# First unit's products ahead of the second unit's scans, counts behind the last unit's products, and fewer dummy matmuls

## The chip, the cores and the metric

The kernel runs on one core of one Trainium2 chip. The metric is the device time of one execution in microseconds; the time of a kernel is the median over its runs. TensorE (PE), VectorE (DVE), ScalarE (ACT), GpSimd (POOL) and SyncE (SP, which here only issues loads) each work through a queue of their own in order, and wait for each other through semaphores.

## The reference

A linear attention with decay over 4 sequences of 768 tokens and 8 heads of 48, then a routed mixture of 8 experts of equal capacity, then a gated second layer:

```python
for t in range(S):
    cur = np.einsum('bhd,bhe->bhde', u[None] * kt, vt)
    y[:, :, t] = np.einsum('bhd,bhde->bhe', rt, state + cur)
    state = wt[:, :, :, None] * state + np.einsum('bhd,bhe->bhde', kt, vt)
...
logits = x @ w_gate                  # the highest scores first, each expert takes at most N/E tokens
h = np.maximum(x[mask] @ w1[e], 0.0)
out[mask] = h @ w2[e]
...
h = x @ w_in
g = h * np.clip(h + 3.0, 0.0, 6.0) / 6.0
return g @ w_out
```

## The kernel before

The attention is cut into 24 units (6 chunks of 128 tokens by 4 sequences; unit n is chunk n // 4 of sequence n % 4). A loop over n writes out one stage per unit by hand, and the order in which a stage calls its helpers is the order of each engine's queue. A unit goes through these helpers:

- `scans(n)` on DVE: a reversed running product `Q` of the decays, the chunk's whole decay `G`, a reciprocal, and the forward scan `Ap`. It is called two stages ahead.
- `khrh(n)`: `kh` = keys times `Q`, `rh` = queries times `Ap`, each on POOL or DVE. `bonus(n)`: `rk` = keys times queries.
- `cc(n)` on PE: the bonus term from `rk`, into the PSUM tile `pu`, of which there is one; `cc_ev(n)` on ACT copies it out.
- `tr(n)` (transposes of `kh`) and `vp(n)` (values times gate weights) on PE, into the PSUM tile `pk`, of which there is one; `vp_ev(n)` and `tr_ev(n)` on ACT copy it out.
- `scores(n)` on PE: products of `kh` and `rh` into two PSUM tiles `sc`; `scores_ev(n)` on DVE masks them into `P`.
- `seed(n)` on ACT starts the output tile `py` (two of them) with the bonus; `ymm(n)` on PE adds the state's part and `P` times the values; `umm(n)` on PE makes the state's update, `sadd(n)` on DVE adds it, `decay(n)` on POOL scales the state.
- `logits(n)` on DVE sums the gate's part of `py`; `xev(n)` on ACT copies the output, `xst(n)` stores it. `check(n)` on ACT looks at the range of the decays (two passes, line 226 and 227).

Stage n calls, on PE: dummy matmuls, `tr(n)`, `vp(n)`, `scores(n)`, then `ymm(n-1)`, `umm(n-1)` and `cc(n+1)`. The dummies multiply a tile of ones (`wz`) into `pk`, where the next products overwrite them; their number per stage stands in `WARMS` (line 65), the last entry for all later stages, and with three more from unit 20 on (line 408). Ahead of the loop, 13 dummies run while the first loads come in, and units 0 and 1 are prepared.

The routing needs counts of tokens by score and expert. `compare8(u)` on DVE writes a comparison `cm` for 128 tokens, `top` on DVE the best expert `oh`, and `sum8(u)` on PE adds their product into `cnt` (two small matmuls each, line 629). The list `counted` holds those that wait for their `sum8`; it is emptied at the end of the stages 22 and 23 and behind the loop's two extra stages 24 and 25.

Behind the loop every engine branches around `stepwise` (line 518), a path for decays out of range. Then the experts' part begins: the search for the thresholds of the first expert on DVE and PE (its first step is `sat`, line 688), the gather of its tokens, and a long stretch of matmuls for 8 experts in which PE is busy nearly all the time. Second-layer weights are decoded on the side: ACT takes an absolute value (line 862), POOL clamps it (line 865).

Of the kernel before, what the change touches and what calls it, by code (L numbers as in the profile page):

```python
# [9 lines left out]
F32 = mybir.dt.float32  # L10
# [5 lines left out]
ALU = mybir.AluOpType  # L16
# [3 lines left out]
B, H, S, D = 4, 8, 768, 48  # L20
CH = 128
NCH = S // CH
NU = B * NCH
# [7 lines left out]
R = 112  # L31
CW = NP * (CH + 1) + 1
# [29 lines left out]
LASTWAIT = 24  # L62
KEPT = 16
COUNT8 = {22: (16, 17), 23: (18, 19), 24: (), 25: ()}
WARMS = 0, 6, 3, 6, 5, 5, 5, 5, 4
F64LO = 2.0 ** -15
F64HI = float(np.uint32(0x47EFFFFF).view(np.float32))

# [1 line left out]
class Kernel:  # L70
# [77 lines left out]
    def attention(self):  # L148
        tc, nc, t = self.tc, self.nc, self.t
        with ExitStack() as ctx:  # L150
# [6 lines left out]
            ps_k = ctx.enter_context(tc.tile_pool(name="ps_k", bufs=1, space=PSUM))  # L157
# [9 lines left out]
            KH = [A.tile([128, NP, CH], F32, name=f"KH{i}") for i in range(3)]  # L167
            RH = [A.tile([128, NP, CH], F32, name=f"RH{i}") for i in range(3)]
# [3 lines left out]
            T = {}  # L172

            def ok(q):
                return 0 <= q < NU
# [24 lines left out]
            def scans(n):  # L200
                d = T[n]
                w = d["w"]
                Q = d["Q"] = wk.tile([R, CW], F32, tag="Q", name=f"Q{n}", bufs=2)
                Ap = d["Ap"] = wk.tile([R, CW], F32, tag="Ap", name=f"Ap{n}", bufs=2)

                nc.vector.tensor_tensor_scan(Q[:, ::-1], w[:, ::-1], top[:R, 0:1].to_broadcast([R, CW]), 1.0, op0=ALU.mult, op1=ALU.min)
                d["G"] = io.tile([R, NP], F32, tag="G", name=f"G{n}", bufs=8)
                nc.vector.scalar_tensor_tensor(d["G"], Q[:, 1:CW - 1:CH + 1], 1.0e-30, top[:R, 0:1].to_broadcast([R, NP]), op0=ALU.max, op1=ALU.mult)
                yield

                nc.vector.reciprocal(w[:, 0:CW - 1:CH + 1], d["G"])
                yield
                nc.vector.tensor_tensor_scan(Ap[:, 0:CW - 1], w[:, 0:CW - 1], top[:R, 1:2].to_broadcast([R, CW - 1]), 1.0, op0=ALU.mult, op1=ALU.add)

            def khrh(n, eng, eng2=None):
                d = T[n]
                d["kh"], d["rh"] = KH[n % 3], RH[n % 3]
                q = d["Q"][:, 1:CW].rearrange("p (a b) -> p a b", b=CH + 1)[:, :, 1:]
                a = d["Ap"][:, 0:CW - 1].rearrange("p (a b) -> p a b", b=CH + 1)[:, :, :CH]
                eng.tensor_tensor(d["kh"][:R], d["kr"][:, 0], q, op=ALU.mult)  # L220
                (eng2 or eng).tensor_tensor(d["rh"][:R], d["kr"][:, 1], a, op=ALU.mult)

            def check(n):
                jk = wk.tile([R, NP, CH], BF16, tag="jk", name=f"jk{n}", bufs=2)
                wv = T[n]["w"][:, 0:CW - 1].rearrange("p (a b) -> p a b", b=CH + 1)[:, :, 1:]
                nc.scalar.activation(jk, wv, AF.Relu, bias=cb[:, 0:1], scale=-1.0, accum_out=acc[:, 2 * n:2 * n + 1])
                nc.scalar.activation(jk, wv, AF.Relu, bias=cb[:, 1:2], scale=1.0, accum_out=acc[:, 2 * n + 1:2 * n + 2])

            def bonus(n):

                d = T[n]
                d["rk"] = wk.tile([R, NP, CH], F32, tag="rk", name=f"rk{n}")
                (nc.vector if n < 2 else nc.gpsimd).tensor_tensor(d["rk"], d["kr"][:, 0], d["kr"][:, 1], op=ALU.mult)

            def cc(n, pu):
                d = T[n]
                d["pc"] = pu[:, 448:448 + H]
                for p in range(NP):
                    nc.tensor.matmul(pu[:, 448 + 2 * p:450 + 2 * p], d["rk"][:, p], UB[:, 2 * p:2 * p + 2], start=True, stop=True)
# [6 lines left out]
            def seed(n):  # L246

                d = T[n]
                py = d["py"] = ps_y.tile([128, H, XW], F32, tag="py", name=f"py{n}")
                for h in range(H):  # L250
                    nc.scalar.activation(py[:, h], d["vx"][:, h], AF.Copy, scale=d["cc"][:, h:h + 1])

            def vp(n, pk):
                for a in range(3):
                    nc.tensor.matmul(pk[:, 448:512], T[n]["vT"][:, a], WG[:, a], start=(a == 0), stop=(a == 2))

            def vp_ev(n, pk):
                nc.scalar.activation(T[n]["vx"][:, :, D:], pk[:, 448:512].rearrange("p (h e) -> p h e", e=E), AF.Copy)

            def tr(n, pk):  # L260
                for p in range(NP):
                    nc.tensor.transpose(pk[:, p * R:(p + 1) * R], T[n]["kh"][:R, p], self.ident[:R, :R])

            def tr_ev(n, pk):
                T[n]["kt"] = wk.tile([128, NP, R], F32, tag="kt", name=f"kt{n}", bufs=2)
                nc.scalar.activation(T[n]["kt"].rearrange("p a b -> p (a b)"), pk[:, :NP * R], AF.Copy)

            def scores(n):
                d = T[n]
                d["sc"] = [ps_s.tile([128, 4, CH], F32, tag="sc", name=f"sc{n}_{i}") for i in range(2)]  # L270
                for h in range(H):
                    p, j = divmod(h, 2)
                    s = slice(64 * j, 64 * j + 64)
                    nc.tensor.matmul(d["sc"][j][:, p], d["kh"][s, p], d["rh"][s, p], start=True, stop=True)

            def scores_ev(n):
                d = T[n]
                d["P"] = []
                for i in range(2):
                    Pm = wk.tile([128, 4, CH], F32, tag=f"P{i}", name=f"P{n}_{i}", bufs=2)  # L280
                    nc.vector.tensor_tensor(Pm, d["sc"][i], mask.unsqueeze(1).to_broadcast([128, 4, CH]), op=ALU.mult)
                    d["P"].append(Pm)
# [34 lines left out]
            def logits(n):  # L317
                nc.vector.tensor_reduce(self.L[:, n], T[n]["py"][:, :, D:].rearrange("p h e -> p e h"), axis=AX.X, op=ALU.add)
# [47 lines left out]
            warm(WARM)  # L366
            for i in range(4):
                nc.gpsimd.memset(Sb[i], 0.0)
            for n in range(2):
                for _ in scans(n):  # L370
                    pass
                khrh(n, nc.gpsimd, nc.vector)
            for i in range(2):
                first = ps_y.tile([128, H, XW], F32, tag="py", name=f"first{i}")
                nc.tensor.matmul(first.rearrange("p a b -> p (a b)"), wz[:, :128], wz[:, :H * XW], start=True, stop=True)
            bonus(0)
            bonus(1)
            pu = ps_u.tile([128, 512], F32, tag="pu", name="pu_")
            cc(0, pu)
            check(0)  # L380
            check(1)
            done = 0
            self.bad = self.P.tile([1, 1], I32, name="bad")
            bs = A.tile([R, 2], F32, name="bs")
# [5 lines left out]
            for n in range(NU + 2):  # L390
# [12 lines left out]
                if n == KST:  # L403
                    self.load_constants()

                if ok(n):
                    pk = ps_k.tile([128, 512], F32, tag="pk", name=f"pk{n}")
                    for _ in range(WARMS[min(n, len(WARMS) - 1)] if n < NU - B else WARMS[-1] + 3):
                        nc.tensor.matmul(pk, wz[:, :128], wz, start=True, stop=True)
                if n < NU - B:  # L410
                    tr(n, pk)
                if ok(n):
                    vp(n, pk)
                    scores(n)
                if n == NU - 1:
# [17 lines left out]
                    bits = self.io_bits(turn[n])  # L433
                if ok(n) and n < 2:
                    scores_ev(n)
                if ok(n - 2):
                    logits(n - 2)
                sg = scans(n + 2) if ok(n + 2) else iter(())
# [10 lines left out]
                if n < 1:  # L449
                    khrh(n + 2, nc.gpsimd, nc.vector)  # L450
# [20 lines left out]
                if ok(n) and n:  # L471
                    vp_ev(n, pk)
                    if n < NU - B:
                        tr_ev(n, pk)
                    seed(n)
                if ok(n + 2):
                    check(n + 2)
                for i in his:
# [4 lines left out]
                if n in AHEADK:  # L483
                    i = n + 2 if n < 3 else n + 1
                    khrh(i, nc.gpsimd, nc.vector if i in RHDVE else None)
# [5 lines left out]
                if ok(n + 2):  # L491
                    bonus(n + 2)
# [9 lines left out]
                if n >= NU:  # L502
                    for i in range(EARLY + 2 * (n - NU), EARLY + 2 * (n - NU) + 2):
                        self.io_abs(i)
                        self.io_clamp(i)
                if n >= NU - 2:
                    for c in counted:
                        self.sum8(*c)
                    counted = []
# [781 lines left out]
```

## Time and profile before

| what | us |
|---|---|
| runs | 898.15, 899.45, 905.95 |
| median | 899.45 |
| profiled execution, its own time | 900.43 |
| its span, first to last instruction | 898.6 |
| PE busy | 844.7 (94%) |
| DVE busy | 523.4 (58%) |
| ACT busy | 426.6 (47%) |
| POOL busy | 464.1 (52%) |
| mean granted clock of TensorE | 0.961 |

A busy share is an average over the whole span: DVE with 58% is nearly always busy in the attention and seldom later. [...] The attention takes about the first 195 us, the first expert's search and gather the next 35.

### The profile page before, as it was taken

How to read it: one execution, taken by the hardware profiler on the slowest of the kernel's cores; microseconds unless marked ns; L12 is line 12 of the kernel's file. 1: busy time of each engine (PE TensorE's matmuls, PEld its weight loads, DVE VectorE, ACT ScalarE, POOL GpSimd, SP SyncE). 2: the span in 40 equal slices, each digit the busy share in tenths (PEclk: the TensorE clock that was granted, in tenths of full speed). 3: DMA queues.
4: the chain of work that ended last, by engine and by line, in shares of the span. 5: the costliest groups of instructions: out<-in, count | busy, mean ns of one | idle time of the engine just before them, and what ended most of it. 6: DMA issues, size and time to landing. Idle time of an engine off the chain costs nothing.

```text
span 898.6 us, 15952 instructions
## 1 busy us (share of the span) xinstructions
PE 844.7 (94%) x5942; PEld 790.1 (88%) x5942; DVE 523.4 (58%) x1269; ACT 426.6 (47%) x1025; POOL 464.1 (52%) x428
## 2 busy tenths in 40 slices
PE   7999999964669999999999999999999999999996
PEld 4889998852568899999999999999999999999996
DVE  6879998847798765654563655355455622422211
ACT  4777777731445453444344443434444353344332
POOL 4558898744673553346337423723662383365232
PEclk7999999975779999999999999999999999999999
DMA  9997777124610050023004101300320130122000
GB/s 251 255 262 224 214 220 225 48 62 173 200 47 1 1 168 27 1 89 106 1 3 132 61 1 54 123 19 1 110 85 1 53 114 27 54 62 80 1 1 27
DMA packets 40343, 80.48 MB, mean 90 GB/s; under 512 B 4416, under 2 KB 20160, under 8 KB 40256
## 3 DMA queue, kind: packets, MB, share of 16 engines
q1 hardware_dynamic: 32576, 62.06, 23.2%
q0 software_dynamic: 3072, 9.44, 3.2%
q10 hardware_dynamic: 4608, 7.87, 2.5%
q8 instruction: 49, 0.80, 0.4%
q14 instruction: 38, 0.31, 0.1%
HBM read 69.91 MB, written 9.44 MB: 88 GB/s over the span
## 4 chain that ended last, share of the span: by engine, by line
PE 62%; DVE 7%; issue 4%; POOL 2%; ACT 1%; DMA 0%; POOLq 0%; ACTq 0%; DVEq 0%
PE pg L980 20%; PE ph L980 10%; PE py L1031 7%; PE py L1029 6%; PE py L1030 6%; PE pa L1004 3%; PE pa L1006 3%; PE pa L1005 3%; POOL gl L1021 1%; DVE q L883 1%; DVE cm L669 1%; PE cnt L679 1%; PE px L966 1%; DVE q L881 1%; POOL io L897 1%
## 5 line engine op out<-in xcount | busy, mean ns | idle before, releaser
L1021 POOL TENSOR_TENSOR gl<-r,gh 128x384 fp32r<-128x384 f32 x126 | 131.9, 1047 | 263.7 <-ACT gh L1020 263.4
L980 PE MATMUL pg<-xh,io 128*128 128x384 f32 x768 | 160.5, 344 | 0.0
L1017 DVE SCALAR_TENSOR_TENSOR r<-r,pg 128x384 f32<-128x384 f32 x128 | 70.6, 552 | 139.7 <-ACT r L1016 138.3
L933 POOL TENSOR_TENSOR wl<-we,wh 128x768 fp32r<-128x768 f32 x60 | 115.4, 1925 | 57.4 <-ACT wh L932 38.4
L980 PEld LDWEIGHTS pg<-xh,io 128*128 128x128 f32 x768 | 131.8, 188 | 2.2 <-ACT xh L1048 1.6
L1031 PE MATMUL py<-io,gl 128*128 128x384 f32 x384 | 130.7, 340 | 1.7 <-POOL gl L1021 1.6
L1029 PE MATMUL py<-io,gh 128*128 128x384 f32 x384 | 131.3, 342 | 0.0
L1030 PE MATMUL py<-io,gh 128*128 128x384 f32 x384 | 129.0, 336 | 0.0
L1016 ACT ACTIVATE r<-pg,three 128x384 f32<-128x384 f32 x128 | 74.3, 580 | 110.0 <-PE pg L980 108.3
L1020 ACT ACTIVATE gh<-r 128x384 fp32r<-128x384 f32 x128 | 67.2, 525 | 104.1 <-DVE r L1017 104.1
L980 PE MATMUL pg<-xl,io 128*128 128x384 f32 x384 | 87.6, 336 | 0.0
L1031 PEld LDWEIGHTS py<-io,gl 128*128 128x128 f32 x384 | 72.0, 188 | 5.2 <-POOL gl L1021 4.9
L998 DVE SCALAR_TENSOR_TENSOR hl<-ph,hh 128x384 fp32r<-128x384 f32 x62 | 34.4, 555 | 71.8 <-ACT hh L997 71.8
L932 ACT ACTIVATE wh<-we 128x768 fp32r<-128x768 f32 x64 | 53.6, 838 | 40.0 <-PE pa L1006 22.6
L1029 PEld LDWEIGHTS py<-io,gh 128*128 128x128 f32 x384 | 72.2, 188 | 0.2
L1030 PEld LDWEIGHTS py<-io,gh 128*128 128x128 f32 x384 | 72.2, 188 | 0.0
L980 PEld LDWEIGHTS pg<-xl,io 128*128 128x128 f32 x384 | 68.7, 188 | 0.0
L980 PE MATMUL ph<-xh,wh 128*128 128x384 f32 x192 | 67.6, 352 | 0.1
L1006 PE MATMUL pa<-hl,wh 128*128 128x384 f32 x192 | 65.4, 341 | 1.4 <-DVE hl L998 0.7
L1004 PE MATMUL pa<-hh,wh 128*128 128x384 f32 x192 | 66.3, 346 | 0.0
L980 PE MATMUL ph<-xh,wl 128*128 128x384 f32 x192 | 65.8, 343 | 0.0
L1005 PE MATMUL pa<-hh,wl 128*128 128x384 f32 x192 | 65.0, 338 | 0.0
(221 smaller groups left out, 1690.7 us busy)
## 6 DMA issues: line engine op xcount, KB each, us to landing
we<-in_w SPq DMA_DIRECT2D x64, 384.0 KB, 3.1
kr<-in_kr SPq DMA_DIRECT2D x24, 448.0 KB, 6.2
raw<-in_wio SPq DMA_DIRECT2D x24, 384.0 KB, 5.4
w<-in_wp SPq DMA_DIRECT2D x24, 226.2 KB, 6.3
v<-in_ve SPq DMA_DIRECT2D x24, 224.0 KB, 3.0
vT<-in_vT SPq DMA_DIRECT2D x24, 192.0 KB, 5.7
xd<-xt ACTq DMA_DIRECT2D x24, 192.0 KB, 4.7
raw<-in_wio ACTq DMA_DIRECT2D x8, 384.0 KB, 5.0
```

What stands on the lines that cost most here:

```text
L933: eng.tensor_tensor(lo, raw, hi, op=ALU.subtract)
L980: nc.tensor.matmul(ps, w[a][part], x[:, a], start=(n == 0), stop=(n == 8))
L1004: nc.tensor.matmul(pa[d], wh[:, c], hh, start=(f == 0), stop=False)
L1005: nc.tensor.matmul(pa[d], wl[:, c], hh, start=False, stop=False)
L1006: nc.tensor.matmul(pa[d], wh[:, c], hl, start=False, stop=(f == NFT - 1))
L1016: nc.scalar.activation(g, ph, AF.Relu, bias=self.three)
L1017: nc.vector.scalar_tensor_tensor(g, g, 6.0, ph, op0=ALU.min, op1=ALU.mult)
L1020: nc.scalar.activation(gh, g, AF.Copy)
L1021: (nc.vector if last and f >= NGT - 2 else nc.gpsimd).tensor_tensor(gl, g, gh, op=ALU.subtract)
L1029: nc.tensor.matmul(py[q], gh[:, c], w, start=(f == 0), stop=False)
L1030: nc.tensor.matmul(py[q], gh[:, c], v, start=False, stop=False)
L1031: nc.tensor.matmul(py[q], gl[:, c], w, start=False, stop=(f == NGT - 1))
```

## The change

Three edits of the order and one of the number of dummies:

1. Ahead of the loop only unit 0 is scanned first; its `rk` follows on DVE, and its transposes, scores, `cc` and `vp` are issued on PE before unit 1's scans are written. Unit 1's `rk` moves from DVE to POOL, its `rh` and `check(1)` into stage 0.
2. From unit 8 to 19 three dummies run in each stage and not four.
3. Stage 23 has no dummies (it had seven; the units 20 to 22 keep seven).
4. `sum8` is no longer called at the end of stages 22 and 23; what is counted so far goes out at the end of stage 24, behind `ymm(23)`.

PE's queue at its start, before (`first` are two matmuls that touch the `py` tiles, `pu__257` is `cc(0)`, the two rows on `pk_272` are `tr(0)` and `vp(0)`, `sc_...` is `scores(0)`, `pu_304` is `cc(1)`):

```order
L375 MATMUL first_251<-wz 128x448
L239 MATMUL pu__257<-UB,rk_253 128x2 x4
L262 MATMUL pk_272<-ident,KH_136 128x112 x4
L255 MATMUL pk_272<-WG,vT_169 128x64 x3
L274 MATMUL sc_0_280<-RH_139,KH_136 128x128
L274 MATMUL sc_1_281<-RH_139,KH_136 128x128
...
L239 MATMUL pu_304<-UB,rk_255 128x2 x4
```

and now, where `pu__261` is `cc(0)`, `pk_246` is `tr(0)` and `vp(0)`, and `pu_300` is `cc(1)`:

```order
L384 MATMUL first_244<-wz 128x448
L271 MATMUL pk_246<-ident,KH_136 128x112 x4
L283 MATMUL sc_0_251<-RH_139,KH_136 128x128
L283 MATMUL sc_1_252<-RH_139,KH_136 128x128
...
L248 MATMUL pu__261<-UB,rk_240 128x2 x4
L264 MATMUL pk_246<-WG,vT_169 128x64 x3
L248 MATMUL pu_300<-UB,rk_280 128x2 x4
```

`cc(0)`, which needs `rk`, no longer stands ahead of the transposes and the scores.

DVE's queue in the same place, before (`Q_231` and `Ap_232` are unit 0's scans, `Q_240` and `Ap_241` unit 1's, `rk_253` and `rk_255` the two bonus products, `P_0_309` the first half of unit 0's masked scores):

```order
L213 SCALAR_TENSOR_TENSOR Ap_232<-w_167,top 112x516
L221 TENSOR_TENSOR RH_139<-kr_168,Ap_232 112x512
L206 SCALAR_TENSOR_TENSOR Q_240<-w_174,top 112x517
...
L213 SCALAR_TENSOR_TENSOR Ap_241<-w_174,top 112x516
L221 TENSOR_TENSOR RH_140<-kr_175,Ap_241 112x512
L233 TENSOR_TENSOR rk_253<-kr_168 112x512
L233 TENSOR_TENSOR rk_255<-kr_175 112x512
L281 TENSOR_TENSOR P_0_309<-sc_0_280,mask 128x512
```

and now:

```order
L214 SCALAR_TENSOR_TENSOR Ap_232<-w_167,top 112x516
L226 TENSOR_TENSOR RH_139<-kr_168,Ap_232 112x512
L242 TENSOR_TENSOR rk_240<-kr_168 112x512
L207 SCALAR_TENSOR_TENSOR Q_272<-w_174,top 112x517
...
L214 SCALAR_TENSOR_TENSOR Ap_273<-w_174,top 112x516
L290 TENSOR_TENSOR P_0_305<-sc_0_251,mask 128x512
L290 TENSOR_TENSOR P_1_307<-sc_1_252,mask 128x512
L226 TENSOR_TENSOR RH_140<-kr_175,Ap_273 112x512
```

`rk` of unit 0 has moved ahead of unit 1's scans, `rk` of unit 1 has left the queue, and `RH_140` (unit 1) stands behind the masked scores of unit 0.

PE's queue from the end of stage 22 on, before (`pu_2533` is `cc(23)`, `cnt_2564` the counts, `pk_2602` the dummies of stage 23 and then `vp(23)`, `pb` a product for the flag of the decays, `py_2547` is `ymm(22)`):

```order
L239 MATMUL pu_2533<-UB,rk_2493 128x2 x4
L627 LDWEIGHTS scale
L627 MATMUL cnt_2564<-base,scale 128x16
L629 LDWEIGHTS cm_0_905
L629 MATMUL cnt_2564<-oh,cm_0_905 128x8
...
L409 MATMUL pk_2602<-wz 128x512
L255 MATMUL pk_2602<-WG,vT_2104 128x64 x3
L274 MATMUL sc_0_2613<-RH_141,KH_138 128x128
...
L417 MATMUL pb<-one,bs 1x1
L290 MATMUL py_2547<-Sb_133,RH_140 128x112
```

and now (`pu_2521` is `cc(23)`, `pk_2556` is `vp(23)`, `py_2604` is `ymm(23)`, `cnt_2651` the counts):

```order
L248 MATMUL pu_2521<-UB,rk_2481 128x2 x4
L264 MATMUL pk_2556<-WG,vT_2094 128x64 x3
L283 MATMUL sc_0_2560<-RH_141,KH_138 128x128
...
L431 MATMUL pb<-one,bs 1x1
...
L302 MATMUL py_2604<-v_2095,P_1_2589 128x56
L645 LDWEIGHTS scale
L645 MATMUL cnt_2651<-base,scale 128x16
L647 LDWEIGHTS cm_0_905
L647 MATMUL cnt_2651<-oh,cm_0_905 128x8
```

`vp(23)` follows `cc(23)` directly; the 33 counts that stood between them and the four that stood between `ymm(22)` and `ymm(23)` now follow `ymm(23)`. On DVE nothing moves outside the start; on ACT only `check(1)` moves, from ahead of `cc_ev(0)` to behind `seed(0)`; SP's queue is the same.

The diff:

```diff
-WARMS = 0, 6, 3, 6, 5, 5, 5, 5, 4
+WARMS = 0, 6, 3, 6, 5, 5, 5, 5, 3
+LASTWARM = 7
...
+            def kh(n, eng):
...
+            def rh(n, eng):
...
             def khrh(n, eng, eng2=None):
...
+                kh(n, eng)
+                rh(n, eng2 or eng)
...
-                (nc.vector if n < 2 else nc.gpsimd).tensor_tensor(d["rk"], d["kr"][:, 0], d["kr"][:, 1], op=ALU.mult)
+                (nc.vector if n < 1 else nc.gpsimd).tensor_tensor(d["rk"], d["kr"][:, 0], d["kr"][:, 1], op=ALU.mult)
...
-            for n in range(2):
-                for _ in scans(n):
-                    pass
-                khrh(n, nc.gpsimd, nc.vector)
+            for _ in scans(0):
+                pass
+            khrh(0, nc.gpsimd, nc.vector)
+            bonus(0)
...
-            bonus(0)
-            bonus(1)
+
+            pk = ps_k.tile([128, 512], F32, tag="pk", name="pk0")
+            tr(0, pk)
+            scores(0)
             pu = ps_u.tile([128, 512], F32, tag="pu", name="pu_")
             cc(0, pu)
+            vp(0, pk)
             check(0)
-            check(1)
+            for _ in scans(1):
+                pass
+            kh(1, nc.gpsimd)
+            bonus(1)
...
-                if ok(n):
+                if ok(n) and n:
                     pk = ps_k.tile([128, 512], F32, tag="pk", name=f"pk{n}")
-                    for _ in range(WARMS[min(n, len(WARMS) - 1)] if n < NU - B else WARMS[-1] + 3):
+                    for _ in range(WARMS[min(n, len(WARMS) - 1)] if n < NU - B else LASTWARM if n < NU - 1 else 0):
                         nc.tensor.matmul(pk, wz[:, :128], wz, start=True, stop=True)
...
+                if n == 0:
+                    rh(1, nc.vector)
...
+                if n == 0:
+                    check(1)
...
-                if n >= NU - 2:
+                if n >= NU:
                     for c in counted:
                         self.sum8(*c)
                     counted = []
```

## Rows read from the trace of the kernel before

**Rows 1.** Stretches: length, busy PE, PEld, DVE, ACT, POOL, granted clock, DMA share, GB/s

```profile
10.00:11.00 1.00, 0.00 (x0) 0.00 (x0) 0.91 (x2) 0.81 (x2) 0.00 (x0) 0.60 1.10 267
...
16.00:24.00 8.00, 8.00 (x42) 6.12 (x40) 5.32 (x7) 4.50 (x14) 2.41 (x2) 0.51 1.10 278
```

**Rows 2.** Timeline of the start, all engines: start us, us, what [idle before, releaser]

```profile
3.08 0.43 SPq L194 DMA_DIRECT2D ident<-in_cst  x1
...
8.79 1.18 POOL L220 TENSOR_TENSOR KH<-kr,Q 112x512 f32<-112x512 f32 x1 [2.06 <-DVE Q L206]
...
9.15 1.23 DVE L213 TENSOR_TENSOR_SCAN Ap<-w,top 112x516 f32<-112x516 f32 x1
9.15 0.72 ACT L226 ACTIVATE jk<-w,cb 112x512 bf16<-112x512 f32 x1 [1.93 <-DVE w L211]
...
10.47 0.69 DVE L221 TENSOR_TENSOR RH<-kr,Ap 112x512 f32<-112x512 f32 x1
...
11.82 1.87 PE L239 MATMUL pu__257<-UB,rk 112*128 112x2 f32 x8 [4.38 <-DVE rk L233]
...
16.32 2.72 ACT L251 ACTIVATE py<-v,cc 128x56 f32<-128x56 f32 x8
...
17.68 1.86 PE L239 MATMUL pu<-UB,rk 112*128 112x2 f32 x8
17.78 1.29 DVE L281 TENSOR_TENSOR P<-sc,mask 128x512 f32<-128x512 f32 x2 [5.41 <-PE sc L274]
...
21.42 1.27 POOL L233 TENSOR_TENSOR rk<-kr 112x512 f32<-112x512 f32 x1
...
21.90 1.33 DVE L221 TENSOR_TENSOR RH<-kr,Ap 112x512 f32<-112x512 f32 x1
...
23.96 1.16 PE L274 MATMUL sc<-RH,KH 64*128 64x128 f32 x16
```

**Rows 3.** The same view a unit later

```profile
30.17 1.16 PE L274 MATMUL sc<-RH,KH 64*128 64x128 f32 x16
```

**Rows 4.** Loads, by line: size of one, median us from issue to landing

```profile
ident<-in_cst SPq DMA_DIRECT2D x1, 64.0 KB, 5.7
```

**Rows 5.** Timeline of PE in the middle, the dummies of units 7, 8 and 9

```profile
63.21 1.24 PE L409 MATMUL pk<-wz 128*128 128x512 bf16 x5
...
70.74 1.02 PE L409 MATMUL pk<-wz 128*128 128x512 bf16 x4
...
78.06 1.02 PE L409 MATMUL pk<-wz 128*128 128x512 bf16 x4
```

**Rows 6.** Thirteen stretches of one unit each in the middle, columns as in rows 1

```profile
84.47:91.79 7.32, 7.32 (x82) 6.57 (x79) 7.21 (x16) 5.67 (x18) 5.98 (x9) 1.00 0.76 242
...
sum 95.37, PE 95.37 PEld 85.53 DVE 87.97 ACT 74.94 POOL 81.60; mean PE 7.34 PEld 6.58 DVE 6.77 ACT 5.76 POOL 6.28
```

**Rows 7.** Timeline of the attention's end, all engines

```profile
180.13 0.97 PE L629 MATMUL cnt<-oh,cm 128*128 128x8 bf16 x32
...
180.96 3.15 PE L409 MATMUL pk<-wz 128*128 128x512 bf16 x7
...
184.80 1.16 PE L274 MATMUL sc<-RH,KH 64*128 64x128 f32 x16
...
190.88 5.84 POOL L865 TENSOR_SCALAR q<-q 128x384 f32<-128x384 f32 x4 [11.01 <-ACT q L862]
...
191.74 0.22 DVE L318 TENSOR_REDUCE L<-py 128x8 f32<-128x64 f32 x1 [0.49 <-PE py L293]
...
193.89 0.21 PE L629 MATMUL cnt<-oh,cm 128*128 128x8 bf16 x2 [1.96 <-DVE oh L596]
...
197.94 0.18 DVE L688 TENSOR_TENSOR sat<-cnt,rem 128x16 bf16<-128x16 f32 x1 [4.29 <-PEq L518]
```

**Rows 8.** Line 518, the branch around the other path: duration ns min/median/max, start us

```profile
L518 PEldq COMPARE_BRANCH  x1: 3820/3820/3820, 194.0 to 194.0; - x1
```

**Rows 9.** The half microsecond in which the last unit's dummies begin, columns as in rows 1

```profile
180.50:181.00 0.50, 0.50 (x25) 0.50 (x22) 0.00 (x0) 0.19 (x1) 0.00 (x0) 0.88 0.00 0
```

More of the change, by code (lines that the diff above doesn't have):

```diff
@@ L213, in scans @@
                 nc.vector.tensor_tensor_scan(Ap[:, 0:CW - 1], w[:, 0:CW - 1], top[:R, 1:2].to_broadcast([R, CW - 1]), 1.0, op0=ALU.mult, op1=ALU.add)
-            def khrh(n, eng, eng2=None):
[L216 to L221, printed above, removed]
+            def kh(n, eng):
+                d = T[n]
+                d["kh"] = KH[n % 3]
+                q = d["Q"][:, 1:CW].rearrange("p (a b) -> p a b", b=CH + 1)[:, :, 1:]
+                eng.tensor_tensor(d["kh"][:R], d["kr"][:, 0], q, op=ALU.mult)
+            def rh(n, eng):
+                d = T[n]
+                d["rh"] = RH[n % 3]
+                a = d["Ap"][:, 0:CW - 1].rearrange("p (a b) -> p a b", b=CH + 1)[:, :, :CH]
+                eng.tensor_tensor(d["rh"][:R], d["kr"][:, 1], a, op=ALU.mult)
+            def khrh(n, eng, eng2=None):
+                kh(n, eng)
+                rh(n, eng2 or eng)
             def check(n):
@@ L404, in attention @@
                     self.load_constants()
-                if ok(n):
+                if ok(n) and n:
                     pk = ps_k.tile([128, 512], F32, tag="pk", name=f"pk{n}")
-                    for _ in range(WARMS[min(n, len(WARMS) - 1)] if n < NU - B else WARMS[-1] + 3):
+                    for _ in range(WARMS[min(n, len(WARMS) - 1)] if n < NU - B else LASTWARM if n < NU - 1 else 0):
                         nc.tensor.matmul(pk, wz[:, :128], wz, start=True, stop=True)
-                if n < NU - B:
-                    tr(n, pk)
-                if ok(n):
+                    if n < NU - B:
+                        tr(n, pk)
                     vp(n, pk)
```

## The prediction, made before the changed kernel was run

> **What bounds the kernel now.** I read the granted clock and the busy shares in stretches of time first, then the timeline at the places that the diff touches, and the waits there. Over most of the attention and all of the experts' part PE is busy without a gap, so a microsecond saved there counts only if PE saves it or if PE was waiting. There are three places with different limits.
>
> At the start PE sits idle for 4.38 us, from 7.44 to 11.82, because `cc(0)` stands first in its queue and the `rk` that it needs comes behind unit 1's scans on DVE [rows 2]. DVE then waits 5.41 us for unit 0's scores. [...]
>
> In the middle the stages follow each other at PE's pace. With five dummies the next stage's dummies come 7.53 us later, with four 7.32 us later [rows 5]: a dummy is worth 0.21 us, and nothing else sets the pace. PE fills its stretches, DVE comes next with 6.77 us of work per stage in the mean and 7.21 in the heaviest of thirteen [rows 6].
>
> At the end, 33 counts (0.97 us for 32) and seven dummies (3.15 us, at half rate since the clock fell just as they began) stand between `cc(23)` and `vp(23)` [rows 7, 9]. DVE's `logits(23)` waits for PE; the last count goes out at 193.89, PE's branch takes 3.82 us behind it, and the search starts at 197.94 with a wait that is put down to that branch [rows 7, 8]. So here PE's order sets the start of all that follows.
>
> **The start, -7.0 us.** PE's first real work no longer waits for `rk`. What is late next is the load of the identity: issued at 3.08, 5.7 us to landing, so `tr(0)` can start at 8.8 [rows 2, 4]. At half rate `cc(0)`, `tr(0)`, `vp(0)` and `scores(0)` took 17.78 - 11.82 = 5.96 us [rows 2]; in the new order they end at 14.8 at half rate and at 11.8 at full rate. `cc(1)` then needs `rk` of unit 1, now on POOL: `KH` at 8.79 moves by the 0.65 us that `rk` of unit 0 takes ahead of it (taken as an operation like the 0.69 us `RH`), runs 1.18 us, and `rk` 1.27 us, which gives 11.9. From `cc(1)` to `scores(1)` it was 23.96 - 17.68 = 6.28 us at half rate, so 3.14 at full rate. `scores(1)` therefore starts at 11.9 + 3.1 = 15.0 at full rate, or 14.8 + 6.3 = 21.1 at half: 8.9 or 2.9 us earlier than now. DVE is ready for either: `Ap` of unit 1 ends at 9.15 + 0.65 + 1.23 = 11.0, the masked scores (1.29) and `RH` (0.69) follow, 13.0. From there the old chain goes on: 30.17 - 23.96 = 6.21 us to `scores(2)` at PE's full pace [rows 2, 3].
>
> ACT can take some of it back. `check(1)`, two passes of 0.72 us, now stands behind `seed(0)` (2.72 us) and ahead of `cc_ev(1)`, together with `check(2)`; `umm(0)` and `cc(2)` on PE wait for `cc_ev(1)`, because there is one `pu`. With `vp(0)` at 11.8, about a microsecond of copies, the seed and two range tests of some 1.7 us each (estimated from the two passes and their reads), `cc_ev(1)` comes at 18.9; PE would want it between the end of `scores(1)`, 16.2, and the next stage. I take 0.5 us of stall; it can be 0 to 2.7.
>
> Between 2.9 and 8.4 I take 7.0. It is nearer to the full rate, because the clock was still at 1.00 at 8.8, where PE now resumes, and fell only at 10.2 with PE still idle [rows 1]; the 1.4 us below the upper end are one stretch at half rate, like the one of 3.15 us that cost 1.65 us at the end (seven dummies at 0.21 would be 1.5) [rows 5, 7].
>
> One row speaks against moving work to POOL: `RH` took 0.69 us with POOL idle and 1.33 us while POOL's `rk` ran [rows 2]. [...]
>
> **The middle, -2.5 us.** Twelve stages, units 8 to 19, lose one dummy of 0.21 us: 12 x 0.21 = 2.5. DVE is the cover that may go: a stage of 7.11 us holds the mean of 6.77 but not the heaviest of 7.21, which runs 0.1 over; the light stages take that back, since PE needs `P` of a unit only a stage later. Lower end 0, if DVE's waits for PE and PE's for DVE lock at 7.32; I take the full amount because DVE's sum of 87.97 us in thirteen stages would fit 13 x 7.11 = 92.4 [rows 6].
>
> **The end, -4.1 us.** Stage 23 begins with `vp(23)` where the counts began, at 180.0 (one start matmul ahead of the 32 at 180.13). From there to `scores(23)` it was 184.80 - 180.0 = 4.8 us; what stays of it is `vp(23)`, at most the 184.80 - 184.11 = 0.7 us behind the dummies, so `scores(23)` comes 4.0 us earlier. The four counts that stood ahead of `ymm(23)` give 0.1 more (4 x 0.03, from 0.97 / 32) [rows 7]. `logits(23)`, which waits for PE, moves from 191.74 to 187.6, and the tail on DVE behind it, the last count (189.8), the branch and the search (193.8) with it. The moved counts, 46 and the start, take 47 x 0.03 = 1.4 us from about 187.2 and are through before the last count's inputs come; at half rate they would take 2.8 and cost some 0.4. POOL's clamps, 190.88 + 5.84 = 196.7, are fed by ACT behind `logits(22)` and move along to 192.6, still before the search.
>
> The bounds: the clock may fall here all the same, since a falling clock met PE at 180.9 right behind the products of stage 22 and the counts [rows 9], and real work would then run at half rate for some 3.3 us: 1.65 + 0.4 less, so 2.0. Upper end 4.3, with nothing lost and 0.2 for the counts. I take 4.1; the products of `vp`, `scores` and `ymm` now follow without a break. The branch stays at 3.82 us.
>
> **Sum.** 7.0 + 2.5 + 4.1 = 13.6 us. The profiled execution took 900.43, so 886.8; it stands 1.0 above the median of the runs, 899.45, and from that the sum gives 885.9, say 886. Everything behind the search shifts as a block: loads there are issued behind the branch, and PE is full.
>
> **The rivals.**
> - *Half rate at the start to the end of unit 1.* For it: PE is still idle from 7.44 to 8.8, and `cc` and `vp` are small. Against it: the gap is a third of the old one. First term 2.9: 9.5 in all, 890.0.
> - *The clock falls in the last unit.* Stage 23 loses its dummies. Last term 2.0: 11.5 in all, 888.0.
> - *DVE takes over the pace in the middle.* For it: 7.21 of 7.32 in the heaviest stage. Middle term 0: 11.1, 888.4.
> - *The start's gain isn't had.* The DMA engines are full (share 1.10) from 10 to 24 us [rows 1]; if loads are what units 2 to 6 wait for, starting earlier only waits earlier. Against it: the waits in the rows of the start are all for another engine, none for a load [rows 2]. First term 0: 6.6, 892.9.
> - *Slower: three dummies no longer hold the clock.* If it falls once in each of the twelve stages, each fall costs 1.65 us as at the end [rows 7]: 12 x 1.65 = 19.8 against 13.6, 905.7. It decides from 13.6 / 1.65 = 8.2 falls on. Against it: the products between a stage's scores and the next dummies see no dummy in either version, and the clock stood at 1.00 through all of these stretches [rows 6]. [...]
>
> **How the numbers follow.** Forecast 0.50; half rate at the start 0.20; clock falls at the end 0.10; DVE sets the middle 0.10; start's gain lost 0.05; slower 0.05. The range goes from the upper ends, 8.4 + 2.5 + 4.3 = 15.2 (884.2, and a microsecond for the spread of the runs), 883, to the start's loss, 892.5, which leaves out the last two cases. A measurement of this kernel can tell about 1% from no change; 1% is 9.0 us, 890.5. Faster by more: the forecast, both middle rivals, and half of the first, 0.80. Within: the other half and the lost start, 0.15. Slower by more: 0.05 at most.
>
> **What the new profile would show.** Right: `tr(0)` at 8.8, `scores(1)` at 15 to 17 and a granted clock of 1.00 there; stages 8 to 19 at 7.11 us with PE unbroken; `scores(23)` straight behind `vp(23)`; counts in one block behind `ymm(23)`; the search some 13.6 us earlier, at about 184. Wrong: PE waiting for `cc_ev(1)` or for DVE's `P`, the clock at 0.50 in the middle, PE's branch longer than 3.82, or a later search with stretches at half rate that were not there before.

## The result, and the profile after

The changed kernel takes 887.6 us (median; 887.44 to 888.65), the kernel before 898.8 beside it: a ratio of 0.9866, 95% interval 0.9834 to 0.9898; that is 11.2 us at the medians and 13.0 between the two profiled executions (900.43 and 887.44; that of before stands 1.6 above its median here). Some executions of the kernel before and of several below, at a lower mean clock (of before, 921.95 us at 0.938 against 897.69 at 0.966), are over 1.5% longer than the fastest of the same kernel; the ratios leave them out.

The start after, first the stretches (columns as in [rows 1]):

```profile
10.00:11.00 1.00, 1.00 (x18) 0.88 (x14) 1.00 (x2) 0.00 (x0) 1.00 (x2) 1.00 1.07 293
11.00:12.00 1.00, 1.00 (x9) 1.00 (x9) 1.00 (x3) 0.02 (x1) 0.90 (x1) 0.80 1.00 240
...
18.00:19.00 1.00, 1.00 (x10) 0.93 (x8) 0.00 (x0) 0.97 (x5) 0.00 (x0) 0.79 1.06 310
```

and PE's timeline there:

```profile
9.19 0.57 PE L271 MATMUL pk<-ident,KH 112*128 112x112 f32 x4 [2.76 <-DMA ident<-in_cst]
9.70 1.16 PE L283 MATMUL sc<-RH,KH 64*128 64x128 f32 x16
...
14.79 2.72 PE L424 MATMUL pk<-wz 128*128 128x512 bf16 x6
...
18.96 1.16 PE L283 MATMUL sc<-RH,KH 64*128 64x128 f32 x16
...
25.17 1.16 PE L283 MATMUL sc<-RH,KH 64*128 64x128 f32 x16
```

PE waits 2.76 us for the identity instead of 4.38 for `rk` (it stands from 6.43 and not from 7.44), and `scores(0)` runs at a granted clock of 1.00 (1.16 us). The clock falls to 0.50 at about 11.6, though, with PE busy, and comes back at about 18.4 (before it was at 0.50 from 10.2 to 23.9), so that the six dummies take 2.72 us. `scores(1)` starts at 18.96, against 23.96 [rows 2], and `scores(2)` at 25.17 against 30.17 [rows 3]: 5.0 us, and up to unit 7 the distance stays 5.0. In the middle, PE's dummies of units 8 to 10, to be set beside [rows 5]:

```profile
65.74 0.81 PE L424 MATMUL pk<-wz 128*128 128x512 bf16 x3
...
72.84 0.81 PE L424 MATMUL pk<-wz 128*128 128x512 bf16 x3
...
79.95 0.81 PE L424 MATMUL pk<-wz 128*128 128x512 bf16 x3
```

They follow each other by 7.10 or 7.11 us, PE has no gap and the clock is 1.00. The end (timeline, all engines), beside [rows 7]:

```profile
173.15 1.16 PE L283 MATMUL sc<-RH,KH 64*128 64x128 f32 x16
...
179.23 5.85 POOL L883 TENSOR_SCALAR q<-q 128x384 f32<-128x384 f32 x4 [6.96 <-ACT q L880]
...
179.96 0.23 DVE L327 TENSOR_REDUCE L<-py 128x8 f32<-128x64 f32 x1 [0.36 <-PE py L302]
179.97 1.31 PE L647 MATMUL cnt<-oh,cm 128*128 128x8 bf16 x46
...
182.13 0.21 PE L647 MATMUL cnt<-oh,cm 128*128 128x8 bf16 x2 [0.84 <-DVE oh L614]
...
186.31 0.17 DVE L706 TENSOR_TENSOR sat<-cnt,rem 128x16 bf16<-128x16 f32 x1 [4.44 <-PEq L536]
```

The counts stand in one block of 1.31 us behind the last products, the clock stays at 1.00 up to them, and the search starts 11.63 us earlier. By place: 5.0 us at the start; `scores(20)` at 153.21 against 160.80, 2.6 more in the middle; `scores(23)` at 173.15 against 184.80, 4.06 more at the end. The other 1.4 us of the 13.0 came behind the search's start, and the prediction has no term for them.

### The profile page after: what moved, and what is told of

Same layout as the page of the kernel before. It is cut to its first block, busy times and chain, and to the rows that moved or that the text cites. A ratio compares the mean times of both kernels' runs of the same rounds, so it can differ in the third digit from the quotient of the medians.

```text
span 885.6 us, 15913 instructions
## 1 busy us (share of the span) xinstructions
PE 836.6 (94%) x5923; PEld 785.8 (89%) x5923; DVE 521.9 (59%) x1268; ACT 426.3 (48%) x1025; POOL 464.6 (52%) x429
## 4 chain that ended last, share of the span: by engine, by line
PE 62%; DVE 7%; issue 4%; POOL 3%; ACT 1%; DMA 1%; POOLq 0%; SPq 0%; ACTq 0%; DVEq 0%
PE pg L998 20%; PE ph L998 10%; PE py L1049 7%; PE py L1047 6%; PE py L1048 6%; PE pa L1022 3%; PE pa L1024 3%; PE pa L1023 3%; POOL gl L1039 2%; DVE q L901 1%; DVE cm L687 1%; DVE q L899 1%; PE cnt L697 1%; PE px L984 1%; POOL io L915 1%
```

## The experiments

In the tables `s(n)` is the start of `scores(n)` on PE and "search" that of the `sat` row, in us, all read from timelines.

**Each part alone** (the first is a diff against the changed kernel, the others against the kernel before).

```diff
# e1_start
-WARMS = 0, 6, 3, 6, 5, 5, 5, 5, 3
+WARMS = 0, 6, 3, 6, 5, 5, 5, 5, 4
-    ... else LASTWARM if n < NU - 1 else 0):
+    ... else LASTWARM):
-                if n >= NU:
+                if n >= NU - 2:
# e2_middle
-WARMS = 0, 6, 3, 6, 5, 5, 5, 5, 4
+WARMS = 0, 6, 3, 6, 5, 5, 5, 5, 3
-    ... if n < NU - B else WARMS[-1] + 3):
+    ... if n < NU - B else 7):
# e3_end
-    ... else WARMS[-1] + 3):
+    ... else WARMS[-1] + 3 if n < NU - 1 else 0):
-                if n >= NU - 2:
+                if n >= NU:
```

> The kernel before with the edit of the start alone; middle and end as before. My theory, the three edits are worth their own place in time and add up: scores(1) starts near 19.0 us and scores(2) near 25.2 as in the changed kernel, everything behind is shifted by 5.0 us, time 898.8 - 5.0 = 893.8. Rival, the saved time is given back behind: shift of 5 us at scores(2) but under 3 us at the last unit's scores (184.8 before), time above 895.8.

> The kernel before with three dummies in units 8 to 19 alone. My theory: stages of 7.11 us with the clock at 1.00, 2.5 us less, 896.3. Rival, the clock falls when the start is as before: stages longer than 7.32 us at some places, time above 898.

> The kernel before with the edits of the end alone: no dummies in unit 23 and the counts behind ymm(23). My theory: scores(23) at 180.8 instead of 184.8, granted clock 1.00 to the counts, 4.0 us less, 894.8. Rival, the clock falls in the last unit when the phase is that of the kernel before: 2 us less, 896.8.

Ratios to the kernel before: start 0.9947 (0.9894 to 1.0001), middle 0.9979 (0.9935 to 1.0022), end 0.9994 (0.9969 to 1.002). No interval leaves 1 out, so the times don't separate the parts; single times go from 891.48 to 996.53 for e1 and from 894.3 to 917.75 for e2. The profiles separate them in part. All three profiled executions ran at half rate (a granted clock of 0.50) from 8.8 (e1), 11.2 (e2) and 10.8 us (e3) to between 48 and 73, so the start's term isn't read from them. In e2's middle a stage takes 7.10 or 7.11 us, in e1's, with four dummies, 7.32: 0.21 a stage, as forecast. In e3 the clock fell in the last unit, where no dummies are left:

```profile
190.00:191.00 1.00, 1.00 (x12) 1.00 (x11) 0.97 (x5) 0.17 (x1) 0.75 (x1) 1.00 0.00 0
191.00:192.00 1.00, 1.00 (x10) 1.00 (x9) 0.54 (x3) 0.49 (x2) 0.24 (x1) 0.84 0.00 0
192.00:196.00 4.00, 4.00 (x28) 3.62 (x27) 1.41 (x4) 2.79 (x10) 0.00 (x0) 0.50 0.15 53
```

and e3's times fall into two groups, five at 895.55 to 896.49 and six at 900.78 to 903.19 (and two longer ones, 913.84 and 918.17); that the second group is this fall wasn't shown.

**The clock at the start.** Twelve dummies behind the two `first` matmuls fill PE's gap:

```diff
+            warm(12)
```

> The changed kernel with 12 more dummies behind the two first matmuls, so that PE does not sit idle from 6.4 to 9.0 us. My theory, the 2 us missing in the start's term are half rate from 11.6 to 18.4 us, and that comes from the idle gap ahead of it: granted clock 1.00 until scores(1), which starts at 15 to 16 instead of 19.0 us, scores(2) at 22 to 23 instead of 25.2, time 887.6 - 2 to 3 = 884.6 to 885.6. Rival A, the clock falls because the products of unit 0 are small, whatever stands ahead: scores(1) stays at 19 us, time unchanged. Rival B, ACT (two range tests ahead of cc_ev(1)) or DVE takes the gain: scores(1) at 15 to 16, but scores(2) no earlier than 24.5.

Measured: 888.64 us, against 884.6 to 885.6 expected, ratio 0.9853 (0.9803 to 0.9902). In the profiled execution the clock stands at 1.00 throughout the start, and `tr(0)` follows without a wait:

```profile
15.17 1.16 PE L283 MATMUL sc<-RH,KH 64*128 64x128 f32 x16
...
21.78 1.16 PE L283 MATMUL sc<-RH,KH 64*128 64x128 f32 x16
```

`scores(2)` starts 3.4 us earlier than in the changed kernel. Of these, 2.9 are the fall at 11.6 (from `scores(0)` to `scores(2)` it is 12.62 us against 15.47), the rest an earlier `scores(0)`. The bridge is no guard, though: of the five kernels here that have it, the clock held at the start in e4, e6 and e10, and fell at 13.6 in e5, with no gap on PE ahead of it, and at 12.9 in e11, behind a wait of 0.79 us. And in e4 the gain doesn't last: `scores(7)` is at 60.60 (60.39 in the changed kernel). PE's timeline shows where it goes, and ACT's what it waits for:

```profile
38.17 0.48 ACT L332 ACTIVATE xt<-py 128x384 f32<-128x384 f32 x1
40.56 0.37 ACTq L337 DMA_DIRECT2D xd<-xt  x1
...
41.09 0.54 ACT L275 ACTIVATE kt<-pk 128x448 f32<-128x448 f32 x1
...
41.68 2.07 PE L425 MATMUL pk<-wz 128*128 128x512 bf16 x5 [0.80 <-ACT kt L275]
```

```profile
41.00:42.00 1.00, 0.32 (x2) 0.19 (x2) 1.00 (x3) 0.97 (x4) 1.00 (x2) 0.98 1.07 323
42.00:43.00 1.00, 1.00 (x4) 0.29 (x2) 0.96 (x2) 0.90 (x4) 1.00 (x2) 0.50 1.08 292
```

ACT has copied `xt` at 38.65 and stands until 40.56 at its own transfer command (`xst`); `kt` of unit 5 comes 0.80 us too late for PE, and behind that wait the clock falls for 3.4 us. A like wait of 0.87 us comes at unit 3, where ACT stood from 23.7 to 26.0. By the times the hold ends with the landing of a load that nothing in unit 5 needs, that of `v7` (SP's timeline, and the load's row in the DMA view of 31.9 to 32.8, with 8.4 us from issue to landing):

```profile
32.06 0.70 SPq L199 DMA_DIRECT2D v<-in_ve  x1
...
v<-in_ve SPq DMA_DIRECT2D x1, 224.0 KB, 8.4
```

32.06 + 8.4 = 40.46, and the command goes at 40.56. The hold at unit 3 ends in the same way, with `v4`: issued at 17.20, 8.8 us, 26.0, and the command at 26.04. In the changed kernel's own trace the wait ahead of unit 5 is put down to such a load by name:

```profile
39.17 0.34 ACTq L337 DMA_DIRECT2D xd<-xt  x1
39.56 0.22 ACT L267 ACTIVATE v<-pk 128x64 f32<-128x64 f32 x1 [1.28 <-DMA v<-in_ve]
```

`v7`, issued there at 31.51, took 7.6 us and landed at 39.1. Why the command waits for another unit's load was not shown. The DMA engines are full there (share 1.07), so an earlier PE meets loads that haven't landed.

How much of the gain goes is a matter of the execution. e8 (below), without the bridge and with the loads as here, kept its clock at the start and has the same hold before unit 5 (37.95 to 39.93), but no fall behind it (1.00 from 40 to 46):

```profile
15.09 1.16 PE L283 MATMUL sc<-RH,KH 64*128 64x128 f32 x16
...
41.03 1.24 PE L424 MATMUL pk<-wz 128*128 128x512 bf16 x4 [0.88 <-ACT kt L275]
...
58.29 1.16 PE L283 MATMUL sc<-RH,KH 64*128 64x128 f32 x16
```

From `scores(1)` to `scores(7)` it is 41.43 us in the changed kernel, 43.20 in e8 and 45.43 in e4: the holds took back 1.8 us in e8, and in e4 4.0, some of it the fall.

**Two ways around ACT's hold**, both on top of the bridge, and the loads without the bridge:

```diff
# e5_issue_later
                     xev(n - 2)
-                    xst(n - 2)
...
                     check(n + 2)
+                if ok(n - 2):
+                    xst(n - 2)
# e6_loads_later, and e12_loads_alone without the bridge
-KST = 2
+KST = 4
-                    if n == B0 + i * 4 // 3 - 3:
+                    if n == B0 + i * 4 // 3 - 2:
```

> The kernel with twelve bridging dummies, and in each unit ScalarE's own transfer command (the store of the unit two back, xst) stands behind seed and check instead of ahead of vp_ev. Theory: with the bridge, ScalarE stood idle 2.3 us (23.7 to 26.0) and 1.9 us (38.7 to 40.6) at that command, which waits for an earlier transfer; so kt came late, PE's dummies of units 3 and 4 waited 0.87 and 0.80 us, and behind the second wait the clock fell for about 2 us. Without it the scores of unit 3 stand at 28.8 (29.64 with the bridge alone), those of unit 7 at 57 (60.60), no half rate between 40 and 46, and the device time is 884 to 885.5. Rival: DMA is full (share 1.07) and v or vT of those units land too late in any order: unit 7 stays at 60 to 60.6 and the time at 887 to 889.

> The kernel with twelve bridging dummies, the constants (412 KB) loaded two units later and each load of raw (384 KB) one unit later. Theory of the full queue: the 412 KB, some 1.5 us at the 280 GB/s of that stretch, stood ahead of the transfers that ScalarE waits for at 38.7 to 40.6, so this second hold shrinks or goes, while the first (23.7 to 26.0, before the constants' load at 28.2) stays: scores of unit 3 at 29.6 as with the bridge alone, those of unit 7 at 57.5 to 59 (60.60), time 885 to 887. Rival: the hold comes from the order of the commands and not from the bytes ahead: unit 7 at 60 to 60.6, 887 to 889.

> The changed kernel with constants and raw loaded later, without the bridge. Theory: two things have to go to get the start's gain past unit 7: the half rate before the second unit (which comes in some executions of this start and not in others) and ScalarE's hold at its transfer command behind the full queue. With the loads alone the executions with the half rate stay where the changed kernel was (unit 7 at 60.4, 885 to 888), and those without it reach the time of the bridge with late loads (unit 7 at 57.4, 884 to 885): median 884 to 888, scattered more than with the bridge. Rival: the loads alone do it, all runs at 884 to 885 with unit 7 at 57.4 to 58, also with the half rate.

e5 missed: its four times lie between 888.38 and 991.62 and the clock of the profiled execution, the longest, is at 0.50 from 37.5 to 256.0 us. Ahead of that, ACT stood again at the moved command:

```profile
29.29 5.06 ACTq L337 DMA_DIRECT2D xd<-xt  x1
...
34.40 0.18 ACT L253 ACTIVATE cc<-pu 128x8 f32<-128x8 f32 x1 [4.30 <-PE py L302]
...
35.54 0.60 PE L310 MATMUL pu<-v,kt 128*48 128x56 f32 x16 [1.41 <-ACT kt L275]
```

Now everything of the next unit on ACT stands behind it, and PE waits 1.41 us. It is not the same hold: the command itself took 5.06 us, where all other stores in these traces took 0.34 to 0.39. Why, and whether the other three executions had it, was not shown. e6 came out a little better than expected: 884.55 us against 885 to 887, ratio 0.9847 (0.983 to 0.9865), the shortest kernel here with an interval, with `scores(7)` at 57.38 against 57.5 to 59. Its four times, 884.07 to 886.31, lie below the four of the changed kernel, but the intervals of the two ratios overlap. Its hold before unit 5 is 0.9 us instead of 1.9:

```profile
37.58 0.48 ACT L332 ACTIVATE xt<-py 128x384 f32<-128x384 f32 x1
38.92 0.34 ACTq L337 DMA_DIRECT2D xd<-xt  x1
```

and PE waits 0.22 us there at most (unit 4). The command goes at 38.92, and `kr8` landed at 38.87 (issued at 31.07, 7.8 us). `v7` had landed at 37.5, before ACT's copy was done (38.06), so the 0.9 us left are no wait for it; that they are one for `kr8` is read from the times alone. How much of `v7`'s earlier landing is the moved bytes, and how much its own earlier issue (30.29 against 32.06), stays open. In one point the expectation failed: the earlier hold shrank too (`scores(3)` at 28.67, not 29.6), although the built order up to there is the same; that microsecond isn't the edit's, nor is e4's fall behind its wait. Beside e8, `scores(7)` comes 0.9 us earlier. e12 gave 887.95, ratio 0.9859 (0.9776 to 0.9942): late loads alone don't reach e6's time, and its four times, 885.96 to 894.68, scatter as expected. Its profile has the half rate at the start, but a short one (13.2 to 16.7), and `scores(7)` at 58.86. With late loads 42.10 (e12), 42.18 (e6) and 42.59 us (e10) pass from `scores(1)` to `scores(7)`, so holds still cost 0.7 to 1.2 us, not 1.8 or more.

**The middle without dummies, and the last unit.**

```diff
# e7_no_middle_dummies
-WARMS = 0, 6, 3, 6, 5, 5, 5, 5, 3
+WARMS = 0, 6, 3, 6, 5, 5, 5, 5, 0
# e8_last_dummies
-    ... else LASTWARM if n < NU - 1 else 0):
+    ... else LASTWARM):
# e9_counts_ahead
-                if n >= NU:
+                if n >= NU - 2:
```

> The changed kernel with no dummies at all in the units from 8 to 19. If the clock holds, PE would need 0.64 us less a stage than with three, but VectorE is busy about 6.8 of 7.1 us, so it takes over at about 6.9 and the twelve stages bring at most 2.5 us more: scores of unit 20 at 150.7 (153.21 with three). Rival, the prediction's slower case moved to none instead of three: in the waits that open on PE the granted clock falls below 1.00 between 65 and 153, the stage gets longer than 7.11 and the time rises above that of the changed kernel by 5 us or more. The clock row of that stretch decides.

> The changed kernel with the seven dummies of unit 23 back, the counts still behind the products. Theory: in the kernel before, the 46 small counting products ahead of them let the clock fall, so the dummies took 3.15 us; with the counts behind, they run at full rate and cost 7 x 0.213 = 1.5 us, the clock stays at 1.00 to the end of the unit, and the saturation test stands 1.5 us later than in the changed kernel (186.31): of the 4.06 us gained at the end, 2.6 stay. Rival: the dummies come at the place where the clock falls whatever stands ahead of them: 3.1 us lost.

> The changed kernel with the counts of the last units back ahead of the last unit's products (no dummies in unit 23). Theory: of the 4.06 us gained at the end 1.42 are the dummies (measured with the dummies back), and the other 2.6 are the counts and the clock that fell after them. So with the counts ahead the step from the scores of unit 22 to those of unit 23 grows from 5.48 us by the 1.3 of the counts and by the half rate behind them, to 8 or 9 us in all, the granted clock falls to 0.50 within about 1 us of the counts, and the saturation test stands 2.6 us or more later against the scores of unit 22 than in the changed kernel (167.67 to 186.31, 18.64 us). Rival: without the dummies the clock does not fall; then only the 1.3 us of the counts come back.

e7's one execution took 882.11 us: the stages shrank to 6.50 us at a clock of 1.00, with `scores(20)` at 147.67, so in this execution neither VectorE nor the clock took over:

```profile
113.77:120.27 6.50, 6.50 (x76) 6.18 (x75) 6.33 (x13) 5.83 (x19) 5.83 (x7) 1.00 0.74 211
```

e8 took 887.13 and e9 895.13. For the last unit, from `s(22)` to the search, with the clock that each trace shows:

| kernel | counts | dummies in 23 | clock in 23 | s(22) to s(23) | s(22) to search |
|---|---|---|---|---|---|
| before [rows 7, 9] | ahead | 7 | falls at 180.9, back at 184.3 | 9.53 | 22.67 |
| e1_start | ahead | 7 | 1.00 | 7.91 | 21.09 |
| e2_middle | ahead | 7 | 1.00 | 7.90 | 20.99 |
| e8_last_dummies | behind | 7 | 1.00 | 6.90 | 19.71 |
| after | behind | 0 | 1.00 | 5.48 | 18.64 |
| e3_end | behind | 0 | falls at 191.7 | 5.83 | 24.60 |
| e9_counts_ahead | ahead | 0 | falls at 176 | 6.48 | 24.66 |

So of the 4.03 us (22.67 - 18.64), 1.6 are a clock fall that the profiled execution of before had and two others with its order (e1, e2) did not, 1.4 the counts (21.09 - 19.71), and 1.1 to 1.4 the dummies. These shares hold to some 0.4 us: with the order of "after" and the clock at 1.00, e4, e6, e7 and e12 took 18.19 to 18.55 from `s(22)` to the search, and 5.47 or 5.48 to `s(23)` like "after" itself. e9 doesn't show what I expected it to: the step to `s(23)` grew by 1.0, the counts alone, and not to 8 or 9; its 6 us to the search are the half rate to the end of the unit, and e3 has the same 24.6 with the counts behind.

**All of it together.** The bridge, late loads and no dummies in units 8 to 19; then none in 20 to 22 either:

```diff
# e10_all_later_none, on e6_loads_later
-WARMS = 0, 6, 3, 6, 5, 5, 5, 5, 3
+WARMS = 0, 6, 3, 6, 5, 5, 5, 5, 0
# e11_no_dummies_late, on e10_all_later_none
-LASTWARM = 7
+LASTWARM = 0
```

> Twelve bridging dummies at the start, constants and raw loaded later, no dummies in the units from 8 to 19; the end as in the changed kernel. The gains add if they lie in different stretches: the loads later with the bridge give 884.55, and no middle dummies took 6.9 us between the scores of unit 7 and of unit 20; so 877.6, within 876 to 880, scores of unit 7 at 57.4 and of unit 20 at 143.3. Rival: VectorE (busy 6.33 of 6.50 us a stage) takes over where the loads of raw now come later, and 2 to 4 us are lost: 880 to 882.

> As the run before it, and no dummies in units 20 to 22 either (seven in each until now). Theory: 3 x 1.49 = 4.5 us of PE's time go, and products alone hold the clock: 873 to 874, scores of unit 23 at 5.5 to 6 us steps after those of unit 20. Rival: with VectorE waiting and fewer products a unit (no transposes there), PE opens waits, the clock falls in unit 21 or 22 and the half rate takes back the gain or more: 877 to 884.

Both missed. e10's six times are 882.45 and five from 913.8 to 936.45; e11's four lie between 894.86 and 992.18. In e10's profile stages are 6.5 us until unit 12, where PE waits 0.37 us for POOL's `KH`:

```profile
89.91 0.60 PE L271 MATMUL pk<-ident,KH 112*128 112x112 f32 x4 [0.37 <-POOL KH L220]
90.35 1.37 PE L264 MATMUL pk<-WG,vT 128*128 128x64 f32 x6
```

```profile
90.00:91.00 1.00, 1.00 (x8) 1.00 (x9) 0.97 (x4) 0.97 (x3) 1.00 (x2) 0.69 0.53 191
91.00:92.00 1.00, 1.00 (x6) 0.88 (x7) 1.00 (x3) 1.00 (x5) 1.00 (x2) 0.50 0.04 16
...
176.00:189.00 13.00, 12.78 (x72) 10.76 (x73) 7.79 (x15) 5.58 (x17) 6.71 (x6) 0.50 0.42 144
189.00:190.00 1.00, 1.00 (x9) 0.87 (x7) 0.01 (x1) 0.00 (x0) 0.00 (x0) 0.82 0.00 0
190.00:191.00 1.00, 1.00 (x16) 0.89 (x16) 0.00 (x0) 0.88 (x4) 0.00 (x0) 1.00 0.00 0
```

The clock falls behind that wait and stays at 0.50, stages of 12.07 us, until unit 20, the first that has dummies again. e7's execution had a wait of 0.29 us up to 137.5 (there for DVE), and its clock held; it is e7's only time, so whether e7 is as uneven as e10 isn't known. The time of these kernels is a matter of the execution, and none of them is a version to keep; that is e6, by its four times.

## Why the prediction was right, and where not

- **The forecast and the sum.** 886.0 was forecast, 887.6 measured, inside the range, and that it lies so near is in part luck. Of the sum of 13.6 only 11.63 came up to the search; the profiled executions differ by 13.0 because the part behind the search, said to move as a block, gave another 1.4. PE's first transposes there come 13.5 us earlier, with a wait for `xg` of 1.81 instead of 3.15 us. Why this load came sooner was not tried.
- **The start, -7.0, measured -5.0.** This is the term that was mis-sized. The order of events was right: the identity was last (9.19, forecast 8.8), `rk` of unit 1 on POOL met no `RH` (it ended at 11.90, `RH` started at 12.18 and took 0.68 us), `P` of unit 0 no longer waited, and ACT's stall, put at 0.5, was nothing here and 0.32 and 0.21 us at full rate (PE's wait for `cc` in e4 and e8). The failed step is "one stretch at half rate" worth 1.4 us and a clock at 1.00 at `scores(1)` at 15 to 17: there were 6.8 us of half rate, PE busy all through, so the first rival was half true. The argument against that rival, a gap a third of the old one, did not hold either: 2.76 us against 4.38. That the clock made the difference is shown by e4 (15.17 and 21.78) and by e8, whose start is the changed kernel's own code and had no fall: `scores(1)` at 15.09, `scores(2)` at 21.58, 8.6 us ahead of before (the upper end was 8.4), and `scores(7)` 7.1 ahead. So the term's size hangs on an execution's clock, not on the order alone; starts without a bridge reached `scores(1)` at 15.09, 16.76, 18.96, 19.98, 20.32 and 21.64 (e8, e12, after, e9, e7, e1), behind gaps on PE of 2.18, 1.33, 2.76, 1.99, 1.86 and 2.69 us: the clock was kept behind one of the longer gaps and lost behind the shortest.
- **The load-bound rival ("the start's gain isn't had").** I gave it 0.05 because no wait in the rows was for a load. It holds in part, in a form I hadn't seen: what stands until a load has landed is not PE for its data but ACT's own command (`v7` lands at 39.1 and the command goes at 39.17 in the changed kernel). In the changed kernel PE waits nowhere for it up to unit 7; with the clock up at the start it takes back 1.8 us of the earlier `scores(1)` in e8, which stays 2.1 ahead of the changed kernel at unit 7, and 4.0 with the clock fall in e4, which is 0.2 behind. With late loads e6 is 3.0 ahead.
- **The middle, -2.5, measured -2.6.** Shown by e2's stages and the three dummies' spacing. "DVE takes over" was wrong by more than I thought: e7 ran stages of 6.50.
- **The slower rival.** Three dummies held the clock at 1.00 in units 8 to 19 of all seven profiles in which it was up at unit 8. It came with none instead of three: five of six times of e10 lie above 898.8, the median before. The price I gave, a fall of 1.65 us in each stage, was the wrong mechanism: a single fall lasted 99 us in e10, and in e5 three dummies in a stage didn't end one (0.50 from 37.5 to 256.0). Nor does the fall at 180.9, which the price was taken from, speak for this rival: PE was full there [rows 9], and e1 and e2 kept the clock with the same order.
- **The end, -4.1, measured -4.06, partly by luck.** 1.6 us of it, the half rate of the seven dummies in the rows of before, belonged to that execution and not to the order: e1's and e2's traces lack it. And the rival "the clock falls in the last unit" came at 6.0 us in e3 (24.60 against 18.64), not the 2.1 I gave it, since the half rate lasted to the end of the unit (0.50 from 191.7 up to 206). The branch took 3.96 us against 3.82.

## What to carry over

When a wait is taken away from a busy engine, look for the next queue that holds a command in order: here ACT's store stood until another unit's load had landed (at 40.46 in e4, and the command went at 40.56), and with bytes moved out of the full stretch the hold was 0.9 us instead of 1.9 (e6). Price dummies by what they insure, not by their own time: three in a stage cost 0.6 us; with them e6 took 884.07 to 886.31 in four executions, without them e10 took 882.45 in one of six and 913.8 or more in five. The profile of e10 shows one fall that lasted (99 us); the other times have no trace. When single profiles differ by a clock fall, compare the same stretch over several kernels' traces before giving the difference to an edit.

## What I had not expected of the hardware

- The granted clock fell while PE was busy: in the changed kernel at 11.6, 2.4 us after a wait had ended (9.19), and in e3's last unit at 191.7 with no wait in the 7 us ahead.
- The same code at the start kept the clock (e8) or lost it at 8.7 (e9), 8.8 (e1), 9.5 (e7), 11.6 (after) and 13.2 us (e12, with another load order later on); with the bridge it kept it three times and lost it twice, once with no gap ahead.
- Half rate lasted while PE was full with small products: in e10 from 90.4 to 189.4 and in e5, through sixteen units with three or five dummies and gaps of 0.22 us at most, from 37.5 to 256.0; both times it ended in unit 20, the first with seven dummies, 0.1 and 2.3 us behind their end. In e11, with none behind unit 7, it lasted from 40.2 until PE ran out of products at 286. How such a stay begins in one execution and not in another was not settled.
